# The first pair of heads of a routing-attention kernel handled ahead of the others, q's next half asked for behind k, and the last weight words put into the probabilities' storage

## The chip, the core and the metric

The kernel runs on one core of one Trainium2 chip. The metric is device time in microseconds (us), the median of several executions. Four compute engines work side by side, each in the strict order of its own program: TensorE (PE; its weight loads are listed as PEld), VectorE (DVE), ScalarE (ACT) and GpSimd (POOL). SyncE (SP) asks for most transfers, also in program order. The trace was taken from one further execution with the hardware profiler.

## The reference

Two steps. The first is clustered attention over 4 batches, 8 heads, 768 tokens, head size 64. A query sees only the keys that have the same nearest centroid (of 16 per head):

```python
q_assign = np.argmax(np.einsum('bhsd,hcd->bhsc', q_n, c_n), axis=-1)
k_assign = np.argmax(np.einsum('bhsd,hcd->bhsc', k_n, c_n), axis=-1)
mask = q_assign[:, :, :, None] == k_assign[:, :, None, :]
scores = scale * np.matmul(q, k.transpose(0, 1, 3, 2))
scores = np.where(mask, scores, -1000000000.0)
attn = softmax(scores)                      # written out in the reference
return np.matmul(attn, v)
```

The second is an MLP on the 3072 x 512 result: `h = x @ w_in` (512 x 2048), ELU of h, `g @ w_out` (2048 x 512). Inputs are float32 except the MLP's weights, which are float64 and come as pairs of 32-bit words.

## The kernel before

**Blocks and slots.** Attention is cut into 32 blocks: 4 batches, 2 halves of the queries (384 each), 4 pairs of heads. A block's scores stand transposed in PSUM, keys in the partitions: six key tiles (kt) of 128 keys, each for the two heads of the pair. `slot(n)` writes the program for block n: `plain` (the score product), `masked` (a second product that adds 0 or minus 2^80-sized numbers from one-hot cluster assignments), and `exponential` (ACT, into `probs`, which lie in `p_out`), for each kt. The score banks are a ring of three tiles (`ring`), so kt 3 needs the bank that the exponential of kt 0 has read. The slot also does what is left of earlier blocks: `row_sums` and `take_sums` of block n-2, `values(n - 1)` (the product with v, 24 records on PE), `sums_end` and `divide`.

**Telling.** To find the nearest centroids, `similar` multiplies q or k by the centroids of all four pairs (four products that write 32 partitions each), and `assign` on DVE transposes the result, takes the maximum over 16, compares and transposes back: the one-hot matrix `hot_q` or `hot_k`. ACT then copies each half to the other 64 partitions (L452), and for q POOL makes `q_mask` (`mask_q`, L459). `clusters_q` and `clusters_k` write the products at once and return the DVE part, which is placed by calling it. What stands in the list `later` is written when `flush()` is called.

**Loads.** Batch 0 is turned by PE (`turned_by_pe`, L573), from rows that `rows_of` loads; all later q and k are loaded in 128-byte pieces by `in_blocks` (four loads for k of a pair, sixteen for half of q) and turned by DVE. At the start SP asks for the centroids, q of four pairs, k of four pairs, v of block 0 and the second half of q, in this order. PE turns q of all pairs, then the centroids, tells q, turns k of all pairs and tells both halves of k; then comes `slot(0)`, which uses the masks of all heads.

**Weights.** The MLP's words arrive in 16 pieces of 1 MB. A piece needs a free place (`places`) to land; `ask()` asks for as many as there are places. It is decoded by a "begin" (two DVE instructions and one on ACT, L326) and three "joins" (one DVE instruction each); the second join frees the place and asks again. After all pieces come four "sums" on DVE over quarters of `w_out`. `weigh(n)` places these steps: each slot adds `ROOM[n]` us of credit to at most 2.5 left over, and steps are taken while the credit covers their `COST` (begin 1.4, join 1.25, sum 2.2); a begin must lie two slots behind its ask, and no join follows a begin in a slot. The last four entries of `ROOM` belong to the units of the first MLP group, after attention. What is left over then is done by `early_on`.

**MLP.** `unit(k_, u)` makes four times 512 rows of the hidden layer from seven block products, with ELU on ACT, POOL (L737) and DVE (L740); sums of weights for units are made by `w_step` on POOL. `second_product_plain` and `second_product` multiply by `w_out`. This part is the same in both kernels, but for what `weigh` puts on DVE beside the first group.

Of the kernel before, what the change touches and what calls it, by code (L numbers as in the profile page):

```python
# [9 lines left out]
F32 = mybir.dt.float32  # L10
BF16 = mybir.dt.bfloat16
# [50 lines left out]
def main_path(ctx, tc, c, q, k, v, centroids, moe_w_in, moe_w_out, out):  # L62
# [71 lines left out]
    top = early[:, 7488:7512]  # L134
    hot_q = early[:, 7512:7896].bitcast(BF16).rearrange("p (s n) -> p s n", s=2)
    probs = [p_out[:, ts(kt, 2 * HS)].rearrange("p (e n) -> p e n", e=2) for kt in range(NT)]
    probs_all = p_out
# [46 lines left out]
    def rows_of(t, src):  # L184

        n = src.shape[1] // P
        t = t.rearrange("p (h t d) -> p h t d", t=n, h=2)
        nc.sync.dma_start(
            t.rearrange("p h t d -> p h (t d)"), src.rearrange("h (p t) d -> p h (t d)", t=n)
        )  # L190
        return t

    cen, ident = c["cen"], c["ident"]
    nc.sync.dma_start(cen, centroids.rearrange("h c d -> (h c) d"))
    first_q = [
        rows_of(p_out[:, 3072 + HS * pr : 3072 + HS * (pr + 1)], q[0, 2 * pr : 2 * pr + 2, :HS])
        for pr in range(NPR)
    ]
    first_k = [
        rows_of(t, k[0, 2 * pr : 2 * pr + 2]) for pr, t in enumerate(raw_k + kT[1][2:])  # L200
    ]
    load_v(0)
    load_q(0, 1)

# [21 lines left out]
    nc.vector.tensor_scalar(big, big, BIG, None, op0=Alu.mult)  # L226

    work = stage[:, 2]
    sq = work[:, :D]
# [17 lines left out]
    cT = const.tile([P, P], F32, name="cT")  # L247
    count = const.tile([P, 4 * B], F32, name="count")
    counted = 0
# [17 lines left out]
    ]  # L267
    words, asked_in, now = {}, {}, -2
    asked, split, joined = 0, 0, 0
# [97 lines left out]
    def weight_sum(n):  # L367
# [12 lines left out]
    ROOM = (  # L380
        [2.3, 2.6, 3.0, 3.0, 1.4, 1.7, 2.6, 2.6] * (B - 1)
        + [2.3, 2.6, 4.0, 4.0, 3.0, 3.0, 3.0, 3.0]
        + [4.0, 5.0, 5.0, 5.0]
    )
# [191 lines left out]

    for two in range(2):
        ps = ring()
        for e in range(2):
            pr = 2 * two + e  # L580
            for t in range(HT):
                turned_by_pe(ps[:, e, ts(t, P)], first_q[pr], t)
            if e == 0:
                nc.scalar.copy(qT[0][pr], ps[:, e, :HS])
            else:
                nc.vector.tensor_copy(qT[0][pr], ps[:, e, :HS])
    nc.tensor.transpose(o_bank[:, :P], work[:, : 2 * D], ident)
    nc.vector.tensor_copy(cT, o_bank[:, :P])
    clusters_q(0, 0, d_bank)()
    flush()  # L590
    for pr in range(NPR):
        ps = ring()
        for t in range(NT):
            turned_by_pe(ps[:, t // HT, ts(t % HT, P)], first_k[pr], t)
        copy = nc.vector.tensor_copy if pr % 2 else nc.scalar.copy
        copy(kT[0][pr].rearrange("p (h s) -> p h s", h=2), ps[:, :, :HS])
    told = [clusters_k(0, half, ps) for half, ps in ((0, o_bank), (1, d_bank))]
    begun = [ring() for _ in range(3)]
    for kt in range(3):
        plain(0, kt, begun[kt])  # L600
    told[0]()
    flush()
    told[1]()
    ask()


    def slot(n):
# [7 lines left out]
        told = None  # L615
        if at == 1:
            told = clusters_q(b, 1, d_bank)
        elif at == 5 and more:
            told = clusters_q(b + 1, 0, d_bank)
        elif at in (6, 7) and more:  # L620
            told = clusters_k(b + 1, at - 6, d_bank)
# [9 lines left out]
        if n + 1 < len(blocks):  # L631
            load_v(n + 1)
        if at == 0:
            nc.vector.transpose(qT_all[1], raw_q_all)
            if more:
                load_k(b + 1, 0)
                load_k(b + 1, 1)
        elif at == 1 and more:
            load_q(b + 1, 0)
        elif 2 <= at < 6 and more:  # L640
            nc.vector.transpose(kT[(b + 1) % 2][at - 2], raw_k[at % 2])
            if at < 4:
                load_k(b + 1, at)
            elif at == 4:
                nc.vector.transpose(qT_all[0], raw_q_all)
                load_q(b + 1, 1)
        weigh(n)

        if n == 0:
            for kt in range(NT):  # L650
                s = begun[kt] if kt < 3 else ring()
                if kt >= 3:
                    plain(n, kt, s)
                masked(n, kt, s)
                exponential(kt, s)
                if kt == 2:
                    flush()
                elif kt == 3:
                    sums_begin()
            flush()  # L660
            return
        for kt in range(NT):
# [438 lines left out]
    def findings():  # L1101
# [6 lines left out]
        nc.vector.tensor_scalar(ok[:, 1:2], peak[:, 1:2], D_MAX, None, op0=Alu.is_lt)  # L1108
        nc.vector.tensor_scalar(same, count, float(HS // NC), None, op0=Alu.is_equal)
        nc.vector.tensor_reduce(ok[:, 2:3], same, axis=Axis.X, op=Alu.min)  # L1110
# [9 lines left out]
    last_n = len(blocks) - 1  # L1120
    for n in range(len(blocks)):
        slot(n)
# [12 lines left out]
    values(last_n)  # L1135
    sums_end()
    take_sums(last_n - 1)
    divide(last_n - 1)
# [308 lines left out]
```

## Time and profile before

| what | value |
|---|---|
| timed, median of 3 | 924.0 us (923.92 to 924.0) |
| the profiled execution | 922.52 us |
| its span on the core | 920.7 us |
| granted clock of PE | 0.997 |
| start to the first value products (L532) | 28.49 us, PE busy 20.77 |
| attention from there | 316.31 us, PE busy 315.57, DVE 304.87, ACT 237.56 |
| first MLP group's first product | 56.16 us, PE busy 52.10, DVE 39.67 |
| the rest, to 918 us | 517.04 us, PE busy 512.18 |

The span is what the profile covers; the execution's own time adds what lies around it. "Busy" sums the time that an engine's instructions run. Idle time of one engine matters only where the engine that sets the end waits for it.

### The profile page before, as it was taken

How to read it: one execution, taken by the hardware profiler on the slowest of the kernel's cores; microseconds unless marked ns; L12 is line 12 of the kernel's file. 1: busy time of each engine (PE TensorE's matmuls, PEld its weight loads, DVE VectorE, ACT ScalarE, POOL GpSimd, SP SyncE). 2: the span in 40 equal slices, each digit the busy share in tenths (PEclk: the TensorE clock that was granted, in tenths of full speed). 3: DMA queues.
4: the chain of work that ended last, by engine and by line, in shares of the span. 5: the costliest groups of instructions: out<-in, count | busy, mean ns of one | idle time of the engine just before them, and what ended most of it. 6: DMA issues, size and time to landing. Idle time of an engine off the chain costs nothing.

```text
span 920.7 us, 15833 instructions
## 1 busy us (share of the span) xinstructions
PE 900.6 (98%) x6080; PEld 686.5 (75%) x6083; DVE 672.9 (73%) x980; ACT 412.1 (45%) x811; POOL 207.4 (23%) x201
## 2 busy tenths in 40 slices
PE   7999999999999998999999999999999999999996
PEld 5444444444444447899988998999899989998996
DVE  4899999999999995772289953595359535953574
ACT  2777687777777773320133223322332233223321
POOL 1112020231303463850024102310231023102200
PEclk9999999999999999999999999999999999999999
DMA  6774564354425221110198762176217621762172
GB/s 166 220 189 88 135 155 87 127 101 90 115 82 141 94 86 69 68 47 1 58 288 307 257 198 60 46 255 195 66 46 255 198 64 45 252 203 64 44 224 81
DMA packets 143331, 121.22 MB, mean 132 GB/s; under 512 B 88208, under 2 KB 104592, under 8 KB 142224
## 3 DMA queue, kind: packets, MB, share of 16 engines
q1 hardware_dynamic: 142000, 115.93, 42.9%
q0 software_dynamic: 1248, 4.20, 1.5%
q8 instruction: 50, 0.82, 0.4%
q14 instruction: 33, 0.27, 0.1%
HBM read 100.96 MB, written 18.09 MB: 129 GB/s over the span
## 4 chain that ended last, share of the span: by engine, by line
PE 77%; DVE 15%; issue 3%; POOL 2%; ACT 1%; SPq 1%; DMA 1%; DVEq 0%; POOLq 0%; ACTq 0%
PE bank L910 22%; PE bank L726 21%; PE o_bank L532 8%; PE banks L494 8%; PE o_bank L910 4%; PE o_bank L726 4%; PE d_bank L910 2%; DVE sums_w L524 2%; DVE sums_w L519 2%; PE banks L507 2%; PE d_bank L726 2%; PE d_bank L550 2%; DVE sums_w L525 1%; POOL kq_g L737 1%; PE banks L573 1%
## 5 line engine op out<-in xcount | busy, mean ns | idle before, releaser
L516 ACT ACTIVATE p_out<-banks 128x768 f32<-128x768 f32 x192 | 154.3, 811 | 25.2 <-PE banks L507 21.2
L737 POOL TENSOR_SCALAR kq_g<-kq_g 128x512 f32<-128x512 f32 x96 | 71.4, 753 | 397.9 <-ACT kq_g L736 397.5
L532 PE MATMUL o_bank<-p_out,kq_g 128*64 128x384 f32 x768 | 129.3, 486 | 0.0
L532 PEld LDWEIGHTS o_bank<-p_out,kq_g 128*64 128x64 f32 x768 | 55.1, 137 | 68.8 <-issue 63.4
L740 DVE SCALAR_TENSOR_TENSOR kq_g<-kq_g,bank 128x512 f32<-128x512 f32 x72 | 48.2, 683 | 72.2 <-POOL kq_g L737 72.2
L726 PE MATMUL bank<-xT,w_in 128*128 128x256 f32 x384 | 90.7, 379 | 0.1
L568 POOL TENSOR_TENSOR xT<-xT,sums_w 128x384 f32<-128x384 f32 x32 | 35.9, 1120 | 203.4 <-DVE sums_w L565 176.1
L726 PEld LDWEIGHTS bank<-xT,w_in 128*128 128x128 f32 x384 | 72.6, 190 | 10.1
L726 PE MATMUL bank<-xT,spare 128*128 128x256 f32 x288 | 67.7, 386 | 3.6 <-ACT bank L778 3.6
L726 PE MATMUL bank<-x_sum,w_in 128*128 128x256 f32 x288 | 68.0, 379 | 0.0
L726 PEld LDWEIGHTS bank<-xT,spare 128*128 128x128 f32 x288 | 55.7, 194 | 11.7 <-POOL kq_g L737 4.0
L524 DVE TENSOR_TENSOR sums_w<-sums_w,p_out 128x1536 f32<-128x1536 f32 x32 | 61.4, 1918 | 3.3
L910 PE MATMUL bank<-w_out,kq_g 128*128 128x128 f32 x512 | 62.9, 275 | 0.0
L910 PEld LDWEIGHTS bank<-w_out,kq_g 128*128 128x128 f32 x512 | 60.4, 192 | 0.3
L519 DVE TENSOR_TENSOR sums_w<-p_out 128x1536 f32<-128x1536 f32 x32 | 58.9, 1842 | 2.0 <-ACT p_out L516 2.0
L726 PEld LDWEIGHTS bank<-x_sum,w_in 128*128 128x128 f32 x288 | 54.6, 190 | 7.3
L736 ACT ACTIVATE kq_g<-bank 128x512 f32<-128x512 f32 x72 | 41.9, 598 | 39.3 <-PE bank L726 39.1
L970 DVE TENSOR_TENSOR kq_g<-kq_g 128x1024 f32<-128x1024 f32 x36 | 43.7, 1221 | 5.3 <-PE bank L910 5.3
L459 POOL TENSOR_SCALAR kq_g<-w_out,big,minus 128x768 bf16<-128x768 bf16 x16 | 32.7, 2052 | 59.1 <-ACT w_out L452 59.1
L494 PE MATMUL banks<-kq_g 64*128 64x384 f32 x192 | 39.7, 492 | 0.7 <-ACT p_out L516 0.7
L494 PE MATMUL banks<-x_sum,xT 64*128 64x384 f32 x192 | 39.6, 493 | 0.6 <-ACT p_out L516 0.6
L494 PE MATMUL banks<-kq_g,xT 64*128 64x384 f32 x192 | 39.6, 491 | 0.0
(233 smaller groups left out, 1707.5 us busy)
## 6 DMA issues: line engine op xcount, KB each, us to landing
spare<-w_far SPq DMA_DIRECT2D x60, 256.0 KB, 2.7
kq_g<-in_v_dram SPq DMA_DIRECT2D x32, 384.0 KB, 3.6
sums_w<-far_s_s SPq DMA_DIRECT2D x40, 256.0 KB, 4.0
words_w<-far_s_s SPq DMA_DIRECT2D x29, 256.0 KB, 3.4
words_w<-in_moe_w_out_dram SPq DMA_DIRECT2D x6, 1024.0 KB, 5.0
out_dram<-p_out SPq DMA_DIRECT2D x24, 256.0 KB, 2.6
w_out<-in_q_dram SPq DMA_DIRECT2D x112, 48.0 KB, 2.4
words_w<-far_a_s SPq DMA_DIRECT2D x21, 256.0 KB, 3.5
```

Of the source, the lines that this page charges most:

```text
L494: nc.tensor.matmul(s[:, e, :HS], lhsT=kT[b % 2][pr][rows, ts(kt, P)], rhs=qT[half][pr][rows], start=True, stop=False,)
L516: nc.scalar.activation(probs[kt], s[:, :, :HS], Act.Exp, scale=SCALE)
L519: nc.vector.tensor_tensor(add_to, probs_all[:, : 4 * HS], probs_all[:, 4 * HS : 8 * HS], op=Alu.add)
L524: nc.vector.tensor_tensor(add_to, add_to, probs_all[:, 8 * HS :], op=Alu.add)
L532: nc.tensor.matmul(o_bank[64 * e : 64 * e + 64, :HS], lhsT=v_raw[n % 2][:, e, kt], rhs=probs[kt][:, e], start=(kt == 0), stop=(kt == NT - 1),)
L568: nc.gpsimd.tensor_tensor(x_of(n), x_of(n), r_of, op=Alu.mult)
L726: nc.tensor.matmul(bank[:, ts(f, QS)], lhsT=left[:, ch, ts(f, P)], rhs=right[:, ch], start=first and f == 0 and ch == 0, stop=ch == 1, ski ...
L736: nc.scalar.activation(to, bank.rearrange("p (f n) -> p f n", f=2), Act.Exp)
L737: nc.gpsimd.tensor_scalar(to, to, 1.0, 0.0, op0=Alu.min, op1=Alu.max)
L740: nc.vector.scalar_tensor_tensor(to, to, -1.0, bank.rearrange("p (f n) -> p f n", f=2), op0=Alu.add, op1=Alu.max)
L910: nc.tensor.matmul(bank[:, :P], lhsT=left[:, f], rhs=right[:, f], start=first and f == 0, stop=last and f == 3, skip_group_check=True,)
L970: nc.vector.tensor_tensor(b[to][:, f], b[x][:, f], b[y][:, f], op=op)
```

## The change

Four things are done, all of them in the order of the program.

1. Loads of batch 0 go pair by pair: q of pair 0, k of pair 0, q of pair 1 and so on, and v of blocks 0 and 1. k of pairs 2 and 3 land where q's second half lands later, so `load_q(0, 1)` is asked for only in `slot_first`, between `load_k(1, 0)` and `load_k(1, 1)`, ahead of the first word pieces.
2. The first pair is told by itself (`similar_first`, `assign_first`, 32 partitions) and has masks of its own (`hot_first`, `q_first`, by DVE with `of_head`); `slot_first` takes the place of `slot(0)`. The other pairs are turned between, each half through `o_bank` or `d_bank` in turn; the telling of all heads, which the slots from 1 on use, comes after the first pair's score tiles.
3. The telling of q's second half moves from slot 1 to slot 3 in batch 0, its turning by DVE from slot 0 to slot 2, and the loads behind it accordingly. `ROOM` gives no decoding to slots 0 to 2 and less to slot 3; the units after attention get 5, 6, 6, 6 for 4, 5, 5, 5.
4. After the last block's sums two places in `p_out` are offered to the words.

The core of the diff:

```diff
--- before.py
+++ after.py
@@ -133,6 +133,8 @@
     oh = early[:, 7296:7488].bitcast(BF16)
     top = early[:, 7488:7512]
     hot_q = early[:, 7512:7896].bitcast(BF16).rearrange("p (s n) -> p s n", s=2)
+    hot_first = kq_g[:32, :384].bitcast(BF16)
+    q_first = kq_g[:32, 384:768].bitcast(BF16).rearrange("p (e n) -> p e n", e=2)
     probs = [p_out[:, ts(kt, 2 * HS)].rearrange("p (e n) -> p e n", e=2) for kt in range(NT)]
     probs_all = p_out
     add_to = sums_w[:, : 4 * HS]
@@ -192,15 +194,14 @@
 
     cen, ident = c["cen"], c["ident"]
     nc.sync.dma_start(cen, centroids.rearrange("h c d -> (h c) d"))
-    first_q = [
-        rows_of(p_out[:, 3072 + HS * pr : 3072 + HS * (pr + 1)], q[0, 2 * pr : 2 * pr + 2, :HS])
-        for pr in range(NPR)
-    ]
-    first_k = [
-        rows_of(t, k[0, 2 * pr : 2 * pr + 2]) for pr, t in enumerate(raw_k + kT[1][2:])
-    ]
+    first_q, first_k = [], []
+    for pr in range(NPR):
+        heads = slice(2 * pr, 2 * pr + 2)
+        first_q.append(rows_of(p_out[:, 3072 + HS * pr : 3072 + HS * (pr + 1)], q[0, heads, :HS]))
+        to = raw_k[pr] if pr < 2 else raw_q_all[:, ts(pr - 2, S)]
+        first_k.append(rows_of(to, k[0, heads]))
     load_v(0)
-    load_q(0, 1)
+    load_v(1)
 
 
     make_identity(nc, ident)
@@ -225,6 +226,10 @@
     nc.vector.tensor_scalar(minus, big, -BIG, None, op0=Alu.mult)
     nc.vector.tensor_scalar(big, big, BIG, None, op0=Alu.mult)
 
+    of_head = const.tile([P, 4], F32, name="of_head")
+    nc.vector.tensor_scalar(of_head[:, :2], par, BIG, None, op0=Alu.mult)
+    nc.vector.tensor_scalar(of_head[:, 2:], par, -BIG, None, op0=Alu.mult)
+
     work = stage[:, 2]
     sq = work[:, :D]
     ss = const.tile([P, 1], F32, name="ss")
@@ -245,7 +250,7 @@
     for e in range(2):
         nc.vector.tensor_scalar(cen2[:, e], cen, par[:, e : e + 1], None, op0=Alu.mult)
     cT = const.tile([P, P], F32, name="cT")
-    count = const.tile([P, 4 * B], F32, name="count")
+    count = const.tile([P, 4 * B + 1], F32, name="count")
     counted = 0
     r_sum = const.tile([P, len(blocks)], F32, name="r_sum")
     d_sum = const.tile([P, len(blocks)], F32, name="d_sum")
@@ -265,7 +270,7 @@
         (w_out[:, f : f + 2], moe_w_out[f * P : (f + 2) * P].rearrange("(f p) m -> p f m", f=2))
         for f in range(0, FC, 2)
     ]
-    words, asked_in, now = {}, {}, -2
+    words, asked_in, now = {}, {}, 0
     asked, split, joined = 0, 0, 0
 
     places = [(words_w.unsqueeze(1), len(pieces))]
@@ -378,9 +383,10 @@
 
 
     ROOM = (
-        [2.3, 2.6, 3.0, 3.0, 1.4, 1.7, 2.6, 2.6] * (B - 1)
+        [0.0, 0.0, 0.0, 1.4, 1.4, 1.7, 2.6, 2.6]
+        + [2.3, 2.6, 3.0, 3.0, 1.4, 1.7, 2.6, 2.6] * (B - 2)
         + [2.3, 2.6, 4.0, 4.0, 3.0, 3.0, 3.0, 3.0]
-        + [4.0, 5.0, 5.0, 5.0]
+        + [5.0, 6.0, 6.0, 6.0]
     )
     COST = {"begin": 1.4, "join": 1.25, "sum": 2.2}
     steps = []
@@ -574,34 +580,110 @@
                 to[D * h : D * h + D], lhsT=t[:, h, n], rhs=ident, start=True, stop=True
             )
 
-    for two in range(2):
-        ps = ring()
-        for e in range(2):
-            pr = 2 * two + e
-            for t in range(HT):
-                turned_by_pe(ps[:, e, ts(t, P)], first_q[pr], t)
-            if e == 0:
-                nc.scalar.copy(qT[0][pr], ps[:, e, :HS])
-            else:
-                nc.vector.tensor_copy(qT[0][pr], ps[:, e, :HS])
+    def turn(to, t, n):
+
+        for i in range(HT):
+            turned_by_pe(to[:, ts(i, P)], t, n + i)
+
+    def similar_first(t, cols, ps):
+        nc.tensor.matmul(ps[:32, :HS], lhsT=cT[:, :32], rhs=t[0][:, cols], start=True, stop=True)
+
+    def assign_first(hot, ps):
+
+        n = HS // NC
+        r = slice(0, 32)
+        nc.vector.transpose(sim[r], ps[r, :HS])
+        s = sim[r].rearrange("p (n c) -> p n c", c=NC)
+        nc.vector.tensor_reduce(top[r], s, axis=Axis.X, op=Alu.max)
+        nc.vector.scalar_tensor_tensor(
+            oh[r].rearrange("p (n c) -> p n c", c=NC),
+            s,
+            1.0,
+            top[r].unsqueeze(2).to_broadcast([32, n, NC]),
+            op0=Alu.mult,
+            op1=Alu.is_equal,
+            accum_out=count[r, 4 * B :],
+        )
+        nc.vector.transpose(hot, oh[r])
+
+    begun = [ring() for _ in range(3)]
+    turn(begun[0][:, 0], first_q[0], 0)
+    nc.scalar.copy(qT[0][0], begun[0][:, 0, :HS])
     nc.tensor.transpose(o_bank[:, :P], work[:, : 2 * D], ident)
     nc.vector.tensor_copy(cT, o_bank[:, :P])
-    clusters_q(0, 0, d_bank)()
-    flush()
-    for pr in range(NPR):
-        ps = ring()
-        for t in range(NT):
-            turned_by_pe(ps[:, t // HT, ts(t % HT, P)], first_k[pr], t)
-        copy = nc.vector.tensor_copy if pr % 2 else nc.scalar.copy
-        copy(kT[0][pr].rearrange("p (h s) -> p h s", h=2), ps[:, :, :HS])
-    told = [clusters_k(0, half, ps) for half, ps in ((0, o_bank), (1, d_bank))]
-    begun = [ring() for _ in range(3)]
+    for h in range(2):
+        turn(begun[1][:, h], first_k[0], HT * h)
+    nc.scalar.copy(kT[0][0].rearrange("p (h s) -> p h s", h=2), begun[1][:, :, :HS])
+    similar_first(qT[0], slice(0, HS), d_bank)
+    for h in range(2):
+        similar_first(kT[0], ts(h, HS), begun[2][:, h])
+    assign_first(hot_q[:32, 0], d_bank)
+    for e in range(2):
+        nc.vector.tensor_scalar(
+            q_first[:, e],
+            hot_q[:32, 0],
+            of_head[:32, e : e + 1],
+            of_head[:32, 2 + e : 3 + e],
+            op0=Alu.mult,
+            op1=Alu.add,
+        )
+    for h in range(2):
+        assign_first(hot_first[:, ts(h, HS)], begun[2][:, h])
+    at_bank = [o_bank, d_bank]
+    for pr in range(1, NPR - 1):
+        for to, t, n in (
+            (qT[0][pr], first_q[pr], 0),
+            (kT[0][pr][:, :HS], first_k[pr], 0),
+            (kT[0][pr][:, HS:], first_k[pr], HT),
+        ):
+            turn(at_bank[0], t, n)
+            nc.scalar.copy(to, at_bank[0][:, :HS])
+            at_bank.reverse()
     for kt in range(3):
         plain(0, kt, begun[kt])
-    told[0]()
-    flush()
-    told[1]()
-    ask()
+
+    def masked_first(kt, s):
+        for e in range(2):
+            nc.tensor.matmul(
+                s[:, e, :HS],
+                lhsT=hot_first[:, ts(kt, P)],
+                rhs=q_first[:, e],
+                start=False,
+                stop=True,
+            )
+
+    def slot_first():
+
+        for kt in range(3):
+            masked_first(kt, begun[kt])
+            exponential(kt, begun[kt])
+        pr = NPR - 1
+        for to, t, n in (
+            (qT[0][pr], first_q[pr], 0),
+            (kT[0][pr][:, :HS], first_k[pr], 0),
+            (kT[0][pr][:, HS:], first_k[pr], HT),
+        ):
+            turn(at_bank[0], t, n)
+            nc.vector.tensor_copy(to, at_bank[0][:, :HS])
+            at_bank.reverse()
+        load_k(1, 0)
+        load_q(0, 1)
+        load_k(1, 1)
+        ask()
+        told = clusters_q(0, 0, d_bank)
+        for kt in range(3, NT):
+            s = ring()
+            plain(0, kt, s)
+            masked_first(kt, s)
+            exponential(kt, s)
+        told()
+        told = [clusters_k(0, half, ps) for half, ps in ((0, o_bank), (1, d_bank))]
+        flush()
+        told[0]()
+        sums_begin()
+        flush()
+        told[1]()
+        flush()
 
 
     def slot(n):
@@ -613,7 +695,7 @@
         if n > 0:
             values(n - 1)
         told = None
-        if at == 1:
+        if at == (1 if b else 3):
             told = clusters_q(b, 1, d_bank)
         elif at == 5 and more:
             told = clusters_q(b + 1, 0, d_bank)
@@ -630,15 +712,18 @@
 
         if n + 1 < len(blocks):
             load_v(n + 1)
-        if at == 0:
+        if at == 0 and b:
             nc.vector.transpose(qT_all[1], raw_q_all)
-            if more:
-                load_k(b + 1, 0)
-                load_k(b + 1, 1)
-        elif at == 1 and more:
+        if at == 1 and b and more:
             load_q(b + 1, 0)
+        if at == 0 and more:
+            load_k(b + 1, 0)
+            load_k(b + 1, 1)
         elif 2 <= at < 6 and more:
             nc.vector.transpose(kT[(b + 1) % 2][at - 2], raw_k[at % 2])
+            if n == 2:
+                nc.vector.transpose(qT_all[1], raw_q_all)
+                load_q(1, 0)
             if at < 4:
                 load_k(b + 1, at)
             elif at == 4:
@@ -646,19 +731,6 @@
                 load_q(b + 1, 1)
         weigh(n)
 
-        if n == 0:
-            for kt in range(NT):
-                s = begun[kt] if kt < 3 else ring()
-                if kt >= 3:
-                    plain(n, kt, s)
-                masked(n, kt, s)
-                exponential(kt, s)
-                if kt == 2:
-                    flush()
-                elif kt == 3:
-                    sums_begin()
-            flush()
-            return
         for kt in range(NT):
             s = ring()
             plain(n, kt, s)
@@ -1106,7 +1178,7 @@
         nc.vector.tensor_reduce(peak[:, 1:2], d_sum, axis=Axis.X, op=Alu.add)
         nc.vector.tensor_scalar(ok[:, 0:1], peak[:, 0:1], -R_MAX, None, op0=Alu.is_gt)
         nc.vector.tensor_scalar(ok[:, 1:2], peak[:, 1:2], D_MAX, None, op0=Alu.is_lt)
-        nc.vector.tensor_scalar(same, count, float(HS // NC), None, op0=Alu.is_equal)
+        nc.vector.tensor_scalar(same, count[:, : 4 * B], float(HS // NC), None, op0=Alu.is_equal)
         nc.vector.tensor_reduce(ok[:, 2:3], same, axis=Axis.X, op=Alu.min)
         nc.vector.tensor_reduce(ok[:, 3:4], ok[:, 0:3], axis=Axis.X, op=Alu.min)
 
@@ -1118,7 +1190,8 @@
         nc.vector.tensor_copy(c["go"], ps[:1, :1])
 
     last_n = len(blocks) - 1
-    for n in range(len(blocks)):
+    slot_first()
+    for n in range(1, len(blocks)):
         slot(n)
         if n == 3 * NB + 1:
             places.append((early[:, 6144:].unsqueeze(1), into + 6))
@@ -1134,6 +1207,9 @@
     row_sums(last_n - 1)
     values(last_n)
     sums_end()
+    for n in range(2):
+        places.append((p_out[:, ts(n, 2048)].unsqueeze(1), len(pieces)))
+    ask()
     take_sums(last_n - 1)
     divide(last_n - 1)
     take_values(last_n)
```

## The prediction

> **What bounds the kernel now.** I read the page first, then TensorE's waits over the start and over the turn from attention to the MLP, then the timeline there.
>
> The page: TensorE (PE) is busy 98% of the span, and of the 40 slices only the first, the 16th and the last are below 9.
>
> ```profile
> span 920.7 us, 15833 instructions
> PE 900.6 (98%) x6080; PEld 686.5 (75%) x6083; DVE 672.9 (73%) x980; ACT 412.1 (45%) x811; POOL 207.4 (23%) x201
> PE   7999999999999998999999999999999999999996
> ```
>
> The windows view (PE busy, then PEld, DVE, ACT, POOL) says where PE is not busy: 7.7 us in the first 28.5, 0.7 in the 316 us of attention, 4.1 in the first MLP group. DVE works 305 of those 316 us: it is a second bound right beside PE, and a step added to it there is not free.
>
> ```profile
> 0.00:28.49 28.49, 20.77 (x205) 13.65 (x206) 16.00 (x41) 10.75 (x17) 2.69 (x9) 1.00 0.73 210
> 28.49:344.80 316.31, 315.57 (x2115) 146.49 (x2114) 304.87 (x338) 237.56 (x385) 84.70 (x56) 1.00 0.47 118
> 344.80:400.96 56.16, 52.10 (x232) 44.07 (x233) 39.67 (x51) 20.45 (x37) 34.72 (x34) 0.97 0.21 73
> ```
>
> The timeline of the start: turning by PE, the telling of k's first half (L436 to L449; the next begins 2.31 us later), the first values at 28.49.
>
> ```profile
> 3.84 1.55 PE L573 MATMUL banks<-ident,p_out 128*64 128x128 f32 x12 [3.84 <-DMA p_out<-in_q_dram]
> 12.59 2.84 PE L573 MATMUL banks<-ident,w_out 128*64 128x128 f32 x48
> 20.45 0.58 DVE L436 STREAM_TRANSPOSE w_out<-o_bank 128x384 f32<-128x384 f32 x1 [0.93 <-PE o_bank L423]
> 22.76 0.54 DVE L436 STREAM_TRANSPOSE w_out<-d_bank 128x384 f32<-128x384 f32 x1
> 28.49 4.09 PE L532 MATMUL o_bank<-p_out,kq_g 128*64 128x384 f32 x24
> ```
>
> The timeline of the turn: the last words are asked at 360.24, because their buffer is emptied only then; DVE waits for them, ACT (strictly in order) waits for DVE, and PE for ACT.
>
> ```profile
> 360.24 0.37 SPq L296 DMA_DIRECT2D words_w<-in_moe_w_out_dram  x1
> 365.30 0.69 DVE L316 TENSOR_SCALAR w_out<-words_w 128x1024 uint32<-128x1024 uint32 x1 [3.53 <-DMA words_w<-in_moe_w_out_dram]
> 366.63 1.15 ACT L326 ACTIVATE sums_w<-sums_w,off 128x1024 uint32<-128x1024 uint32 x1 [5.42 <-DVE sums_w L324]
> 369.37 3.52 PE L726 MATMUL bank<-xT,spare 128*128 128x256 f32 x8 [3.58 <-ACT bank L778]
> ```
>
> **Part 1, the start.** What counts is when PE begins the values of block 1, since PE hardly waits afterwards. Before, that is 39.20 in the chain; slot 1 holds the telling of q's second half (d_bank L423, 0.78), which moves to slot 3, so the mark to beat is 38.42.
>
> The path in the changed kernel, with before's durations. PE turns q's first pair at 3.84: 12 records, 1.55 at the slow early pace. Then cT's transpose, to 6.0. k's first pair, now second in the queue, is there by 5.6 to 6.2 (before, as many bytes had landed at 6.2). Its 24 records take 2.83, to 8.8. ACT copies (0.75). Meanwhile one similarity product, then two for k: all three write the same 32 columns, so they can't lie side by side like the four of L423 (0.78 together); I take 0.64 each at full pace, 1.28 slow. That ends at 11.4 if the pace rises at 10.0 (below).
>
> From there PE does not wait: six turns of 12 records (24 took 1.48, so 0.74 each) 4.44; three plain products at 0.65, 1.95; three first masks, 0.96 (0.16 per product, and both heads use the same 32 rows, so in turn, where the old masks overlapped); three more turns 2.22; q's similarities 0.80; kt 3 to 5 at 0.97, 2.91; k's two halves 1.60. The last ends at 26.3. Values of block 0 thus start at 26.3 against 28.56: 2.2 us earlier.
>
> Most of that is given back in slot 1. k's first half can be told only from 25.7 (its similarities come after kt 5). DVE then runs a telling (2.31), sums_begin (L519, 1.8), a telling (2.31), with one gap closed, to 32.2; ACT's two copies L452 (1.03), take_values (0.49) and the first exponential (0.74, as three took 2.20) follow in ACT's order, to 34.5. PE has kt 3's bank free only then, and was there at 26.3+3.87+3x0.81 = 32.6: a new wait of 1.9. From 34.5 three kt (2.43) and row sums (0.80): values of block 1 at 37.7. Gain 0.7.
>
> Two unknowns. First, the pace. The turns' matmuls take 421 ns at the median until 10.5 and 272 from 12.6, although the granted clock reads 1.00 throughout. Before, 5.9 us of PE work (1.55+2.83+1.51) had been done when it rose; the changed kernel, nearly gapless from 6.0, has done that by 10.0, the value taken. No earlier than 8.8 (before's longest unbroken stretch, 2.83, was not enough): gain 1.0. If as late as 12.6: loss 0.5. [...]
>
> Second, POOL. mask_q (L459) now runs beside sums_begin. Before, POOL's pair took 1.95 with DVE idle and 3.65 beside L524 and L525, which rose from 1.76 to 2.35 and from 0.96 to 1.55. So 0 to 0.6 falls on the chain; I take 0.2, as the pair is nearly through when sums_begin starts. [...]
>
> Start: 0.5 gained (bounds -1.1 and +1.0).
>
> **Part 2, slots 1 to 31.** Decoding is put off (ROOM 0,0,0,1.4 where it was 2.3,2.6,3.0,3.0), so the first slots have DVE to spare. SP: load_k(1,0), then load_q(0,1) (eight after k's pair 2 is turned at 16, eight after pair 3 at 21), load_k(1,1), the three 1 MB word loads, and only then load_v(2). At 0.66 per q and 0.83 per k (the paces at 37.39 and 55.97) SP reaches the words at 30.3. Before, v behind the words landed at 34.0, 13.3 after their issue; so v(2) lands at 43.7, and is wanted at 47.6. Cost 0, by a cover of 3.9 us. qT's second half is transposed in slot 2 and used in slot 4: covered.
>
> By the rules of weigh, begin and three joins fall together in slots 27 and 30, where before it was slot 28, where that cost PE 0.7 (L494 waiting for ACT). Slot 28's wait goes, slot 30's comes (POOL is as busy there): net 0, bounds +0.7 and -1.5.
>
> **Part 3, the last words.** They go to p_out as soon as the last sums are read, near 347, and land near 352 (5.0 us median), where the first use is near 371. The 3.58 goes. What is late next: decoding is one begin and two to three joins behind. Unit 1's weigh does three joins and a begin (1.21+1.63+1.52+1.4 = 5.8, was 4.2 of joins), and the begin's L326 stands on ACT before the copies that PE needs: 0 to 0.7, I take 0.3. Unit 2's weigh does three joins and two sums (4.36+2.28+2.59 = 9.2, was three sums, 7.5); L779 behind it already made PE wait 0.37, so 1.7 more. Unit 3 has two sums (4.9, was 2.3), which end before M2 needs c21: 7.1 us of M1 cover it. Net gain 3.6-0.3-1.7 = 1.6 (bounds -0.5 and +3.6).
>
> **Small edits.** of_head adds two DVE instructions of 0.17 near 2.4, hidden behind the wait for k; the wider count, the slice in findings and load_v(1) at the start (ahead of need by 25 us) cost nothing.
>
> **Sum.** 0.5+0+1.6 = 2.1 us. The profiled execution took 922.5 (span 920.7 and 1.8 around it), the timed median is 924.0, 1.5 above. Taken from the median: 921.9; from the span: 918.6.
>
> **Rivals.** A, more: the pace rises at 8.8, POOL is out of the way, and the later decoding finds slack: 1.0+3.6, 919.4. For it: PE's gaps vanish, and DVE is only 70% busy around the turn. Against: the 0.37 wait on L779 shows no slack there.
>
> B, slower: the SP queue. If q's 16 loads go at 0.90 and k's at 1.68 (before's own paces at 6.20 and 23.15), the words are asked at 37.2, v(2) lands at 50.5, PE waits 2.9 for it in slot 2, and the sum is 924.8; it decides from 47.6 on, each us one for one. For it: 28 small loads and 3 MB stand ahead of v(2), where only v(1) stood behind them. Against: both slow paces were seen while the queue was full of other transfers.
>
> C, the change does not do what it says: block 0 is ahead, but every head's telling still stands before slot 1's exponentials. With the bounds of that chain (pace at 12.6, 0.6 of POOL) and slot 30's wait of 1.5 it eats the turn's gain: -1.1-1.5+1.6, 925.0 at worst, about 924 if half of it comes.
>
> **Chances.** Forecast 0.45, A 0.22, B 0.13, C 0.20. 0.2% is 1.85 us, about what a measurement here can tell from no change. Of the forecast's case somewhat over half lies beyond it (0.26), with A 0.48 faster. B with its further delays (v(3) waits too) and half of C are slower: 0.23. Same: 0.29. The range goes from A's end to B's, with 1.5 us more on each side for the bounds left out: 917.9 to 926.3.
>
> **What would show it.** Right: values of block 0 near 26.3 and of block 1 near 37.7, PE's wait for ACT in slot 1 near 1.9, none for DMA in slot 2; no 3.5 us DVE wait for words, a wait near 2 on L779 in unit 3. Wrong: matmuls at 272 ns before 9 (A); PE waiting for v (B); values of block 1 after 38.4 (C).

## The result and the profile after

The changed kernel is slower: 931.35 us at the median of four (930.3 to 931.87), against 923.96 for the kernel before on the same chip. The ratio is 1.0082, with a 95% interval of 1.0065 to 1.01. The forecast was 921.9, with a range of 917.9 to 926.3.

The page of the changed kernel (span; busy time of each engine; PE and its granted clock in 40 slices) shows little. PE is still busy for 98%, and DVE has 6.3 us more work than before. Only two dips of the clock that is granted to PE stand out, in slices 15 and 18:

```profile
span 929.6 us, 15881 instructions
PE 906.4 (98%) x6089; PEld 688.0 (74%) x6089; DVE 679.2 (73%) x998; ACT 413.1 (44%) x815; POOL 207.3 (22%) x201
PE   8999999999999989979999999999999999999997
PEclk9999999999999989989999999999999999999999
```

The windows view (PE, PEld, DVE, ACT, POOL busy; granted clock) cuts the span as before: up to the first values, attention, first MLP group. The start is 0.9 us shorter. Attention is 7.7 longer and contains 5.4 us in which PE does nothing. The first group is 2.2 longer, with 5.7 of idle PE:

```profile
0.00:27.58 27.58, 22.90 (x211) 13.40 (x211) 15.27 (x48) 12.16 (x19) 0.74 (x7) 1.00 0.64 157
27.58:351.62 324.04, 318.64 (x2113) 147.51 (x2114) 310.55 (x349) 236.27 (x386) 86.39 (x58) 0.99 0.47 120
351.62:409.93 58.31, 52.64 (x234) 44.42 (x233) 41.06 (x52) 21.45 (x38) 34.70 (x34) 0.94 0.19 69
```

**The start.** Six rows of PE's timeline: the first turn, the first similarity, the turns of the other pairs, the values of block 0, the wait in slot 1, the values of block 1.

```profile
4.41 1.55 PE L579 MATMUL banks<-ident,p_out 128*64 128x128 f32 x12 [4.41 <-DMA p_out<-in_q_dram]
9.06 0.83 PE L589 MATMUL d_bank<-x_sum,cT 128*32 128x384 f32 x2
11.43 0.88 PE L579 MATMUL o_bank<-ident,p_out 128*64 128x128 f32 x12
27.58 4.09 PE L538 MATMUL o_bank<-p_out,kq_g 128*64 128x384 f32 x24
35.58 0.92 PE L500 MATMUL banks<-x_sum,xT 64*128 64x384 f32 x4 [1.27 <-ACT p_out L522]
38.89 4.04 PE L538 MATMUL o_bank<-p_out,kq_g 128*64 128x384 f32 x24
```

In this view of the kernel before, the values of block 1 start at 39.03, and the mark for block 1 is 39.03 - 0.78 = 38.25. The changed kernel is 0.64 behind it.

**Slots 30 and 31.** PE has no wait from slot 2 to slot 30; then comes one of 4.12. The timelines of DVE, ACT and PE there (L341, L345 and L351 are the joins; L321, L329 and ACT's L331 the begin; L525 is `sums_begin`; L522 the exponentials):

```profile
330.54 1.22 DVE L341 SCALAR_TENSOR_TENSOR sums_w<-words_w,sums_w 128x1024 uint32<-128x1024 uint32 x1
331.67 2.02 DVE L345 SCALAR_TENSOR_TENSOR w_out<-words_w,w_out 128x1024 f32<-128x1024 uint32 x1
333.73 2.17 DVE L351 SCALAR_TENSOR_TENSOR w_out<-w_out,sums_w 128x1024 f32<-128x1024 f32 x1
335.83 1.75 DVE L321 TENSOR_SCALAR w_out<-w_out 128x1024 uint32<-128x1024 uint32 x1
337.50 0.68 DVE L329 TENSOR_SCALAR sums_w<-w_out 128x1024 uint32<-128x1024 uint32 x1
338.11 1.74 DVE L525 TENSOR_TENSOR sums_w<-p_out 128x1536 f32<-128x1536 f32 x1
```

```profile
326.35 4.85 ACT L522 ACTIVATE p_out<-banks 128x768 f32<-128x768 f32 x6 [0.51 <-PE banks L513]
338.22 1.15 ACT L331 ACTIVATE sums_w<-sums_w,off 128x1024 uint32<-128x1024 uint32 x1 [7.02 <-DVE sums_w L329]
```

```profile
341.76 1.65 PE L500 MATMUL banks<-kq_g 64*128 64x384 f32 x4 [4.12 <-ACT p_out L522]
343.52 1.49 PE L500 MATMUL banks<-kq_g 64*128 64x384 f32 x4
```

DVE takes 7.6 us of decoding in one go, from 330.54 to 338.1, and ACT's part of the begin waits 7.02 for it, with the next exponentials queued behind it. In slot 28 of the kernel before the same three joins and begin took as long, from 306.77 to 314.39, and PE waited 0.74:

```profile
306.77 1.22 DVE L336 SCALAR_TENSOR_TENSOR sums_w<-w_out,sums_w 128x1024 uint32<-128x1024 uint32 x1
313.79 0.68 DVE L324 TENSOR_SCALAR sums_w<-words_w 128x1024 uint32<-128x1024 uint32 x1
318.04 0.92 PE L494 MATMUL banks<-kq_g 64*128 64x384 f32 x4 [0.74 <-ACT p_out L516]
```

In both kernels PE goes on 3.65 after DVE is done with the begin (318.04 - 314.39, 341.76 - 338.11). What differs is when PE's wait began: before, 2.9 after that moment (317.30); now, 0.5 ahead of it (337.64). So DVE is 3.4 us further behind PE than it was. Behind the wait of 4.12, PE's records are slow: 1.49 for four where 0.81 is usual, until 347. The windows view gives PE's granted clock, the first column of two decimals behind the bracketed counts, as 0.50 there, and again behind the second wait:

```profile
341.70:344.00 2.30, 2.24 (x8) 1.32 (x10) 2.16 (x6) 1.64 (x4) 0.00 (x1) 0.50 0.00 0
344.00:346.90 2.90, 2.90 (x14) 1.01 (x10) 2.90 (x3) 1.39 (x2) 1.83 (x1) 0.50 0.00 0
404.40:408.00 3.60, 3.59 (x9) 2.88 (x10) 3.60 (x4) 0.00 (x0) 0.00 (x0) 0.50 0.02 5
```

**The turn.** The 3.53 wait for words is gone. In its place PE waits 5.62 in unit 3 for L851, which stands on DVE behind three joins and two sums (L376, L378) and comes late:

```profile
390.94 1.22 DVE L341 SCALAR_TENSOR_TENSOR sums_w<-p_out,sums_w 128x1024 uint32<-128x1024 uint32 x1
...
395.28 2.58 DVE L376 TENSOR_TENSOR w_out<-w_out 128x2048 f32<-128x2048 f32 x1
397.90 3.24 DVE L378 TENSOR_TENSOR p_out<-w_out 128x2048 f32<-128x2048 f32 x1
...
403.57 0.69 DVE L851 TENSOR_TENSOR o_bank<-o_bank,spare 128x512 f32<-128x512 f32 x1
```

```profile
404.41 3.75 PE L798 MATMUL o_bank<-xT,spare 128*128 128x256 f32 x8 [5.62 <-DVE o_bank L851]
```

Summed against the profile of before: start 0.6; slot 30's wait 4.12 where slot 28 had 0.74, 3.4; slow records behind it 2.5; 5.62 for 3.58 and 0.37, 1.7; slow records 1.9 where before had 1.6 (8 records of L726 in 3.52 for 1.89), 0.2. That is 8.4 of the 8.9 by which the spans differ. (The profiled execution of before, at 922.5, was the shortest of its four, so the spans differ by 1.5 more than the medians.)

### The profile page after: what moved, and what is told of

It reads as the page before. It is cut to its first block, busy times and chain, and to the rows that moved or that the text cites. A ratio compares the mean times of both kernels' runs of the same rounds, so it can differ in the third digit from the quotient of the medians.

```text
span 929.6 us, 15881 instructions
## 1 busy us (share of the span) xinstructions
PE 906.4 (98%) x6089; PEld 688.0 (74%) x6089; DVE 679.2 (73%) x998; ACT 413.1 (44%) x815; POOL 207.3 (22%) x201
## 4 chain that ended last, share of the span: by engine, by line
PE 89%; DVE 7%; ACT 1%; issue 1%; DMA 0%; POOL 0%; SPq 0%; DVEq 0%; ACTq 0%
PE bank L798 23%; PE bank L982 22%; PE banks L500 12%; PE o_bank L538 11%; PE o_bank L798 4%; PE o_bank L982 4%; PE banks L513 3%; PE d_bank L556 2%; PE d_bank L982 2%; PE d_bank L798 2%; PE d_bank L429 1%; DVE sums_w L530 1%; DVE w_out L351 1%; DVE w_out L345 1%; DVE sums_w L525 1%
## 5 line engine op out<-in xcount | busy, mean ns | idle before, releaser
L522 ACT ACTIVATE p_out<-banks 128x768 f32<-128x768 f32 x192 | 153.9, 811 | 33.8 <-PE banks L513 26.7
L809 POOL TENSOR_SCALAR kq_g<-kq_g 128x512 f32<-128x512 f32 x96 | 69.2, 730 | 400.0 <-ACT kq_g L808 399.7
L530 DVE TENSOR_TENSOR sums_w<-sums_w,p_out 128x1536 f32<-128x1536 f32 x32 | 58.6, 1831 | 3.6 <-ACT sums_w L566 0.5
L525 DVE TENSOR_TENSOR sums_w<-p_out 128x1536 f32<-128x1536 f32 x32 | 58.2, 1819 | 2.8 <-ACT p_out L522 2.8
L500 PE MATMUL banks<-kq_g 64*128 64x384 f32 x192 | 41.9, 517 | 4.1 <-ACT p_out L522 4.1
```

The costliest lines, as they stand in the source:

```text
L500: nc.tensor.matmul(s[:, e, :HS], lhsT=kT[b % 2][pr][rows, ts(kt, P)], rhs=qT[half][pr][rows], start=True, stop=False,)
L522: nc.scalar.activation(probs[kt], s[:, :, :HS], Act.Exp, scale=SCALE)
L525: nc.vector.tensor_tensor(add_to, probs_all[:, : 4 * HS], probs_all[:, 4 * HS : 8 * HS], op=Alu.add)
L530: nc.vector.tensor_tensor(add_to, add_to, probs_all[:, 8 * HS :], op=Alu.add)
L809: nc.gpsimd.tensor_scalar(to, to, 1.0, 0.0, op0=Alu.min, op1=Alu.max)
```

## The experiments

Theory T: the time is lost by the placing of the decoding (`ROOM`). DVE is busy for 96% of attention (304.87 of 316.31 us before), so what is taken out of slots 0 to 3 piles up at the end: in slots 27 to 30, and in unit 2. (The units are the four parts of the first MLP group, numbered from 0.) Rivals: the new start and the moved telling (S), or the places in `p_out` (P).

**1 to 4: the parts by themselves.** The four kernels ran on one chip with the kernel before (923.5). The edit of 1 and 2, on the changed kernel:

```diff
     ROOM = (
-        [0.0, 0.0, 0.0, 1.4, 1.4, 1.7, 2.6, 2.6]
-        + [2.3, 2.6, 3.0, 3.0, 1.4, 1.7, 2.6, 2.6] * (B - 2)
+        [2.3, 2.6, 3.0, 3.0, 1.4, 1.7, 2.6, 2.6] * (B - 1)
         + [2.3, 2.6, 4.0, 4.0, 3.0, 3.0, 3.0, 3.0]
-        + [5.0, 6.0, 6.0, 6.0]
+        + [4.0, 5.0, 5.0, 5.0]
     )
```

Experiment 2 takes out these lines too; 3 adds them, and nothing else, to the kernel before; 4 adds them and the new `ROOM` to it:

```diff
+    for n in range(2):
+        places.append((p_out[:, ts(n, 2048)].unsqueeze(1), len(pieces)))
+    ask()
```

> The changed kernel with the ROOM of before (2.3, 2.6, 3.0, 3.0 in the first four slots, 4, 5, 5, 5 after attention); start, telling and places as in the changed kernel. Theory T (the loss comes from the decoding put off, which DVE, busy 97% of attention, can make up only in a back-log that ends in PE's 4.12 wait and the 5.62 wait behind five pieces of decoding in one unit): both long waits and the half-speed records behind them go, a wait below 1 in slot 28 may stay, 922 to 924. Rival S (the new start and the moved telling cost the time, wherever it shows): 929 to 932. Rival P (the places in the probabilities' storage cost it): 929 to 932.

> The changed kernel with the ROOM of before and without the two places in the probabilities' storage: only the start, the loads and the telling are new. T: the start loses 0.6, and the last words are asked even later than before, in the second unit after attention, so a wait of 3.5 to 5 for words stays: 925 to 928. Rival S: 930 or more. Rival P: 924.

> The kernel before with nothing but the two places in the probabilities' storage. T: the wait of 3.58 and the 1.7 of half-speed records behind it go, the decoding stays where it was: 918.5 to 920. Rival P (the wait is replaced by one as long): 923 to 925.

> The kernel before with the ROOM of the changed kernel and the two places: the old start, the new placing of the decoding. T: the 4 us wait in slot 30, the 5.6 us wait in the units and the half-speed records behind both are all there: 929.5 to 931.5. Rival S: 920 to 924.

| | old ROOM | new ROOM |
|---|---|---|
| old start, no places | 923.5 | not run |
| old start, places | 919.05 (experiment 3, ratio 0.9954, 0.9937 to 0.9971) | 929.76 (4, 1.008, 1.0063 to 1.0097) |
| new start, no places | 926.42 (2, 1.0032, 1.0019 to 1.0045) | not run |
| new start, places | 924.55 (1, 1.0009, 1.0 to 1.0019) | 931.35 (the changed kernel) |

All four are at or within 0.6 us of what T expected. The new `ROOM` costs 10.7 us on the old start (929.76 - 919.05) and 6.8 on the new one. The places gain 4.4 on the old start: the wait of 3.58, and the 1.6 of slow records behind it, less a wait in unit 3 that grew by 1.0. P falls. S is not the main cause, but with the old `ROOM` the new start still costs 5.5 (924.55 - 919.05). PE's waits in experiment 4 (us in all, times, longest), on the old start, are the two of the changed kernel:

```profile
PE o_bank L727 <- DVE o_bank L780: 5.7, 1, 5.7
PE banks L495 <- ACT p_out L517: 4.8, 2, 4.2
```

In experiment 3, from 20 us on, none is longer than 1.4:

```profile
PE o_bank L726 <- DVE o_bank L779: 1.4, 1, 1.4
PE banks L494 <- ACT p_out L516: 1.2, 2, 0.6
```

Two limits of this table. The first entries of `ROOM` and its last four were not tried apart. Followed step by step on paper, `weigh` gives the old places with the old first entries and the new last four; with the new first entries and the old last four it gives the same crowded slots 27 to 30, and in unit 2 three joins and one sum instead of two. Neither was run. And the old `ROOM` on the new start is not the old placement: in experiment 1 the first words are asked at 29.31 (before: 20.66) and the first begin comes at 45.58 (before: 26.69), so the decoding ends later, and unit 2 has three joins and a sum where experiment 3 has three sums. T had not expected the wait that came of it in experiment 1, which is part of the 5.5:

```profile
397.76 3.44 PE L797 MATMUL o_bank<-xT,spare 128*128 128x256 f32 x8 [2.35 <-DVE o_bank L850]
```

**5 to 7: one placement at a time, on the changed kernel.** Experiment 5 lets the sums start a unit later:

```diff
-            if kind == "join" and begun or kind == "sum" and n < len(blocks) + 2:
+            if kind == "join" and begun or kind == "sum" and n < len(blocks) + 3:
```

Experiment 6 takes the begin out of slot 30, and 7 does both:

```diff
-        + [2.3, 2.6, 4.0, 4.0, 3.0, 3.0, 3.0, 3.0]
+        + [2.3, 2.6, 4.0, 4.0, 3.0, 3.0, 2.0, 3.0]
```

> The changed kernel with one number changed: the four sums over w_out may start one unit later, so that unit 2 decodes only the last piece (4.4 us on DVE) and the sums come in unit 3 and behind it. T: the 5.62 wait in unit 3 goes, with the 1.9 of half-speed records behind it, less what the sums in unit 3 make late (0 to 3): 924 to 927. Rival (the wait there is POOL's or ACT's, DVE only the last to come): 929 to 931.

> The changed kernel with one entry of ROOM changed, 2.0 for 3.0 in slot 30, so that the begin that stood behind three joins in slot 30 comes in slot 31, and three joins of slot 31 in the first unit; units 1 to 3 as they were. T: the 4.12 wait and the 2.5 of half-speed records go, a wait below 1 may come in the first unit: 924.5 to 926. Rival (the back-log as such makes PE wait, wherever the begin stands): the wait moves by a slot, 929 to 931.

> Both edits together, the begin out of slot 30 and the sums out of unit 2; start, loads and places as in the changed kernel. T: both waits and the half-speed records behind both go, 918 to 920, since the parts add. Rival (what is taken off one place comes back at the next): 924 or more.

Experiment 5: 923.43 (ratio 1.0004, 0.9995 to 1.0014), 7.9 below the changed kernel and a little better than expected. The wait in unit 3 is gone and the records after it are at full speed; the sums in unit 3 make nothing late that PE waits for:

```profile
399.12 1.97 PE L798 MATMUL o_bank<-xT,spare 128*128 128x256 f32 x8
```

Experiment 6: 930.42 (1.0081, 1.0063 to 1.0098), only 0.9 lower. Here T was wrong in part, and the rival half right. The wait at the same place is 2.02, still with slow records behind it, and as PE reaches the units earlier, the begin behind unit 1's joins (ACT's L331 waits 3.60 there) now makes a wait of 1.76 in unit 2. ACT's timeline for slot 31 says what was late next. With the begin gone, the exponentials themselves wait for `sums_begin`, which must have read the probabilities before they are overwritten, and which stands on DVE behind the three joins:

```profile
338.21 2.21 ACT L522 ACTIVATE p_out<-banks 128x768 f32<-128x768 f32 x3 [3.25 <-DVE sums_w L525]
```

So of the 4.12, 2.1 belonged to the begin and the rest to the back-log of joins.

Experiment 7: 922.58 (0.999, 0.998 to 0.9999), with ten runs in two groups: 920.04 to 920.64, and 922.26 to 922.97. The expected 918 to 920 was missed by what experiment 6 showed: a wait of 2.00 in slot 30 and one of 1.76 in unit 2 are left. The mean granted clock is 0.998 in the lower group and 0.996 in the upper one, so the groups differ in slow records; they are why experiment 8 was timed again, as experiment 11.

**8 and 11: a wait of 2 us.** The kernel of experiment 3, with a quarter of the second sum made twice:

```diff
         elif n == 1:
             nc.vector.tensor_tensor(w["s2"], w["s1"], w["a11"], op=Alu.subtract)
+            again = [w[x][:, :2] for x in ("s2", "s1", "a11")]
+            nc.vector.tensor_tensor(*again, op=Alu.subtract)
```

> The kernel before with the two places alone, and a quarter of the second sum over w_out made twice on DVE (about 0.65 more), so that PE's wait of 1.36 in unit 3 becomes about 2.0. After 1.36 the next 8 records took 1.97, after 2.35 (the changed kernel with the old ROOM) 3.44. If the length alone decides and the border is below 2.0, they take about 3.4 here; if it is above, 2.0. Time 919.7 or 921.2.

> The kernel of the 2.04 wait, timed. After both edits together, with a wait of 2.00, three runs were at 920.0 to 920.6 and seven at 922.3 to 923.0. If a wait of 2 sometimes drops the clock and sometimes not, the times here fall in two groups about 1.5 to 2 apart (near 919.5 and 921.3). If 2.04 is below the border, all lie within 919.2 to 920.4.

Experiment 8 took 919.21 in its one execution; experiment 11, the same kernel timed, 920.42 (919.92 to 921.61; ratio 0.997, 0.9958 to 0.9982), spread out rather than in two groups. The two profiles are the finding. First experiment 8, then 11: the same program, the same wait to 0.01 us, and the records behind it at full speed in one and slow in the other:

```profile
393.95 1.97 PE L728 MATMUL o_bank<-xT,spare 128*128 128x256 f32 x8 [2.04 <-DVE o_bank L781]
395.75 1.89 PE L728 MATMUL bank<-x_sum,w_in 128*128 128x256 f32 x8
```

```profile
394.17 3.24 PE L728 MATMUL o_bank<-xT,spare 128*128 128x256 f32 x8 [2.03 <-DVE o_bank L781]
397.21 2.34 PE L728 MATMUL bank<-x_sum,w_in 128*128 128x256 f32 x8
```

Behind the wait of 2.03 the granted clock fell to 0.50, behind that of 2.04 it stayed at 1.00, so the length alone does not decide. The traces show one difference. In all fourteen the granted clock changes only at moments that lie a whole number of times 3.413 us apart (in the kernel before its stretches at one clock, from 10.72 us on, are 358.40, 3.41 and 546.13 us long, 105, 1 and 160 times that; in the changed kernel, from 9.09 on, 331.09, 6.83, 54.61, 6.83 and 518.83, which is 97, 2, 16, 2 and 152 times), and between the start and the last products every stretch at 0.50 is one or two such windows long. Laid on this grid, the wait of experiment 11 falls into one window (391.29 to 394.70, PE busy 1.38 of 3.41 us) and the next window runs at 0.50. That of experiment 8 is cut by the window's start at 392.05, which leaves PE 1.52 of busy time, and the clock stays. The windows view, experiment 8 and then 11:

```profile
392.05:395.47 3.42, 1.52 (x7) 1.40 (x8) 3.42 (x6) 0.54 (x1) 1.20 (x2) 1.00 0.73 204
395.47:398.88 3.41, 3.41 (x24) 3.15 (x23) 2.90 (x3) 1.68 (x3) 2.14 (x3) 1.00 0.35 103
```

```profile
391.29:394.70 3.41, 1.38 (x7) 0.91 (x7) 3.38 (x7) 0.59 (x1) 1.96 (x3) 1.00 0.52 93
394.70:398.11 3.41, 3.41 (x10) 2.66 (x9) 2.71 (x2) 0.66 (x2) 0.00 (x0) 0.50 0.35 138
```

The same holds for experiments 6 and 7, whose waits of 2.02 and 2.00 in slot 30 left 1.40 (slow after it) and 1.48 (not slow). This was read afterwards; no run moved a wait along the grid on purpose.

**9, 10 and 12: the start mended.** `told[1]()` stays where it is on DVE, but ACT's copies for it come later:

```diff
         told[1]()
-        flush()
...
             exponential(kt, s)
+            if n == 1 and kt == 0:
+                later.pop(0)()
```

Experiment 9 does this with the old `ROOM` and the later sums of experiment 5, experiment 10 on experiment 7. Experiment 12 is experiment 3 again.

> The changed kernel with the old ROOM (as in the first experiment, 924.55), the sums from unit 3 on, and ACT's two copies for k's second half put behind slot 1's exponential of kt 0 and behind its last one. T: slot 1's wait of 1.28 goes, and in unit 3 the wait of 2.35 with 1.5 of half-speed records: 924.55 - 1.28 - 3.85 = 919.4, about as the places alone on the old start (919.05). Rival (the new start pays once its wait is gone): 918 or less, faster than the places alone. Rival (DVE, with the added tellings 6 to 7 us busier, gives it back elsewhere): 921 or more.

> As both edits together (922.58), with ACT's two copies for k's second half moved behind slot 1's exponentials. T (slot 1's wait is ACT held by those copies, which wait for DVE): the 1.28 goes and the rest stays, 921.3. Rival (DVE's chain is what counts, and the wait moves into slot 31): 922.6.

> The places alone on the kernel before, once more beside the others, for the comparison: 918.4 to 919.7 as the first time, one group, since its longest wait is 1.36.

Experiment 9: 919.16 (0.9955, 0.9942 to 0.9969), as T expected. Experiment 10: 919.94 (0.9961, 0.9947 to 0.9975), 2.6 below experiment 7 where 1.3 was expected; its wait of 1.99 left the clock alone in the profile, and the times show no upper group. Most of the 2.6 is that: experiment 7's lower group, at 920.4, is only 0.5 above. Experiment 12: 918.85 (0.9955, 0.9941 to 0.9968), as expected, but not its longest wait: in its profile one DVE instruction of unit 2 (L805) took 2.32 instead of 0.69, PE waited 1.87 for what stood behind it, and the 1.36 in unit 3 did not come. PE's waits in experiment 9:

```profile
PE d_bank L428 <- ACT sums_w L565: 1.9, 2, 1.4
PE d_bank L555 <- ACT spare L842: 0.8, 1, 0.8
PE banks L499 <- ACT p_out L521: 0.5, 1, 0.5
PE bank L798 <- ACT bank L850: 0.2, 1, 0.2
```

Slot 1's wait and that in unit 3 are gone, 1.28 and 2.35 with its 1.5 of slow records, which make most of the 5.4 that experiment 9 is below experiment 1. The 1.9 left in the telling products comes where ACT's L331 waits for DVE, 1.3 and 1.0: begins again. Neither rival is borne out: the new start, once mended, stands level with the old one (919.16 against 918.85). The comparison is not pure, since experiment 9 also has the later sums, which the old start was not given; with them it might lose its own wait in unit 3 (1.36 in experiment 3), so what the new start is worth stays open by about that much. Experiments 3 and 9 are faster than both the kernel before and the changed one; of the change, the places in `p_out` are the part to keep.

## Why the prediction was wrong, step by step

**The step that failed most: slot 30 at net 0.** Part 2 named the right slot and the right chain (joins and a begin in one slot, PE waiting for ACT), but took its price from slot 28's 0.7, with 1.5 as the end of the bounds. It was 4.12, and 2.5 of slow records. The price of a crowded slot went with how far behind DVE already was. The decoding itself took 7.6 us in both slots, and beside POOL single DVE instructions were longer in both kernels alike (`sums_begin` 2.83 for 1.75 at the median and the begin's first 1.78 for 0.69 before, 2.83 and 1.75 after). The 3.4 more are DVE's lag behind PE, and the four slots up to there held three more joins: six joins and three begins in slots 25 to 28 before, nine and three in slots 27 to 30 of the changed kernel. The prediction itself had said that DVE works 305 of 316 us. Yet it read `ROOM`'s zeros as "DVE to spare" in the first slots and never asked in which slots the same work would be done instead. Its bounds were too narrow as well: even the three lower ones together (-1.1, -1.5, -0.5) give only 927.1.

**Part 3: the wait in unit 3 at about 2.** The 3.58 did go, and gained more than put down (4.4 by experiment 3), since the 1.6 of slow records behind it were a price that the prediction did not see. The 5.62 that followed comes out as follows. From the first step of unit 2's decoding to L851 it was 12.63, against 10.31 from the first sum to L779 before, so 2.3 for the 1.7 taken (L378 took 3.24, with POOL busy for 2.91 of them beside it). And DVE began it 2.9 later relative to PE. One of these 2.9 is the cover that the removed wait itself had given: in the profile of experiment 3, where nothing but the places is changed, the same wait grows from 0.37 to 1.36 as PE comes earlier. The other 1.9 DVE brings along from unit 1, whose begin holds ACT and with it the ELU; that is read from the timeline and was not tried by itself. 0.37 + 2.3 + 2.9 is 5.6. The one term for length was near; the term for when it begins was missing.

**Part 1: 0.5 gained.** It was 0.64 lost. Values of block 0 came at 27.58, not 26.3. The first q came 0.57 late (4.41 for 3.84), which is chance: the fourteen profiles have it between 3.77 and 4.84 with either order of loads. But it was made up: the similarities ended at 11.43 (11.4 forecast). That agreement is luck. The forecast had the pace rise at 10.0, after 5.9 us of PE's work; it rose at 9.1, after 4.7 (the first similarity took 0.83, not the slow 1.28; k's two, which write the same 32 columns, took 1.48 together, where the four of L429 took 0.85), and in the fourteen profiles it rises after 3.1 to 6.3, so the amount of work is not what decides. So all of the 1.3 came behind the similarities. Of it 0.9 is kt 3 to 5, which took 1.27 each where 0.97 was put down: the scores take 0.85 to their first masks and the masks, whose two products use the same 32 rows, 0.42 to what follows (0.17 for the two of slot 1, on different rows), one after the other. The rest is 0.2 in the plain products, 0.1 in the first masks and 0.2 in the last three turns. Slot 1 took 11.31 from values to values (11.4 forecast), its wait 1.27 (1.9). Over the profiles with the new start as changed, values of block 1 stand at 38.26 to 38.98; with the old start, less 0.78, at 37.75 to 38.25 in five of six. So the loss is real, but small. With ACT's copies moved it is 37.16 and 37.73, a gain of about 0.5; but the three tellings of the first pair are work that DVE did not have before, and the kernel as a whole (experiment 9) is no faster than with the old start (12).

**What held.** Slots 2 to 29 without a wait on PE; v(2) on time, so rival B did not come; the 3.53 wait for words gone. Rival C had the direction (the start gives nothing, and slot 30 eats what the turn gains), but its prices ended at 925.

**The clock.** The waits of 3.58, 4.12 and 5.62 each had half-speed records behind them (granted clock 0.50), which cost 1.6, 2.5 and 1.9 us. The prediction asked for TensorE's pace at the start alone, and not behind the waits that it removed and made. Shorter waits were enough: behind those of 2.02, 2.03 and 2.35 the records were slow as well, with PE busy for 1.40 us (the wait of 2.02) and 1.38 (2.03) of the 3.41 us ahead of the change. An equal wait ended both ways (2.04 and 2.03 in experiments 8 and 11).

## What to carry to other kernels

When the second engine is nearly as full as the first, work that is put off has to be placed again: follow it slot by slot to where it lands, and price a crowded slot by the back-log it meets, not by the same slot elsewhere. A wait that is removed had been cover for what comes next, so move the engine that waited earlier in the timeline before reading off the next cover. Count a wait of 2 us or more on TensorE as the wait and, by what was measured here, up to 2.5 us of half-speed work behind it (1.5 behind 2.35, 1.6 behind 3.58, 2.5 behind 4.12). Waits of up to 1.4 that stood by themselves cost only themselves here, so three of 1, well apart, should cost less than one of 3; that is an estimate from these waits. The same wait had slow records behind it in one profile and none in another (2.03 and 2.04 in experiments 11 and 8), and the ten times of experiment 7 lie in two groups some 2 us apart, so time such a kernel several times.

## What the runs showed of the hardware

- TensorE's clock and waits: after single waits of 1.28, 1.36 and 1.87 the next records were at full speed; after 1.99, 2.00 and 2.04 too; after 2.02, 2.03, 2.35 and all longer ones they were slow. The price was 1.5 to 1.6 us (after 2.35 and 3.58), 1.9 (after 5.62) and 2.5 (after 4.12).
- The grid: in all fourteen traces the granted clock changes at whole multiples of 3.413 us from its other changes, and behind the start it is 0.50 for one or two such windows (for example 369.12 to 372.53 in the kernel before, 340.18 to 347.01 in the changed one). The eleven windows at full clock in which PE was busy for at most 1.40 us were each followed by a slow one; of all the others (1.48 or more) one was (the next point). A border between 1.40 and 1.48 is an inference from these traces; the ends of PE's records are modelled.
- Two shorter waits close together: in one profile of experiment 3 two waits of 0.58 and 0.86 within 2 us in slot 0 were followed by slow records (granted clock 0.88 over 20 to 28 us), and values of block 0 came at 29.59; in the other five profiles with this start they came at 27.98 to 28.49. PE was busy for 1.89 of the 3.41 us of that window, more than the 1.48 above; why it was slow after it stays open.
- POOL beside DVE: the begin's first instruction took 1.75 instead of 0.69 and `sums_begin` 2.82 instead of 1.75 in the slots in which POOL works on the MLP's sums, in both kernels.
